# One-core Fourier mixing and SwiGLU kernel: weight columns loaded by thirds, odd folds moved, od copies and unit order changed

## The chip, the cores and the metric

The kernel runs on one core of a Trainium2 chip. The core has five engines, each with its own stream of instructions: TensorE (PE, matrix products), VectorE (DVE), ScalarE (ACT), GpSimd (POOL) and SyncE (SP, which here only issues transfers). They wait for each other by semaphores, and transfers between the chip's memory (HBM) and the core's memory (SBUF) run beside them on 16 DMA engines. The metric is the device time of one execution in microseconds (us); less is better. Three executions of the kernel before took 606.0, 605.89 and 604.55 us, with a median of 605.89 us.

## The reference

```python
X = np.fft.fft(x, axis=1)            # x: (8, 3008, 256)
X = np.fft.fft(X, axis=2)
h = X.real.reshape(8 * 3008, 256)
g = h @ w_gate                       # (256, 1536)
silu = g * (1.0 / (1.0 + np.exp(-g)))
out = (silu * (h @ w_val)) @ w_out   # (1536, 256)
```

The input is taken through a Fourier transform over the 3008 rows of each of the 8 batches and another over the 256 channels; only the real part is kept. Each of the 24064 resulting rows then goes through a gated block with 1536 hidden columns.

## The kernel before

The real part of the double transform is a product of cosines minus a product of sines. Row k of a batch is P - Q and row M - k is P + Q, with P the cosine part and Q the sine part, so the kernel computes P and Q for half of the rows (12032 of them) and derives both rows of a pair. The channel transform is never applied to the rows: it is multiplied into the weights. On TensorE, 256 x 256 tables of cosines (CD) and sines (SDt) are multiplied with the raw gate and value weights, and the results are copied to Wp and Wq; Wm is Wq times a column m2 that is -2 except at one place. This is done in thirds of 512 of the 1536 columns. The first third is made in the written-out beginning (`first_w`, line 490; `double`, line 499), the other two inside the planned part (`weight_op`, line 1746), one product at a time: gate cosine, gate sine, value cosine, value sine.

The 12032 half rows are cut into 24 tiles of 320 to 512. A unit is a tile t and one of twelve slices f of 128 hidden columns, 288 units in all. In tile 0 and in two units of tile 1 a unit is "whole": gate and value each get a product with Wp on P, one with Wq on Q, and, after SiLU on ScalarE and a product on VectorE (lines 1320 and 1323) have used that sum, one with Wm on Q for the mirrored row (SiLU in line 1341, product in line 1344). All these products are recorded in line 1285. The other units share the work differently (marks in `KINDS`), with products also on GpSimd (lines 1496, 1505 and 1508). The last product with w_out is line 1549, and rows leave by SP's queue (line 1562).

The seven later batches are loaded by SP's queue, folded by GpSimd (lines 174 to 198) and transformed on TensorE (line 1708) while the units of earlier tiles run. Batch 1's part C is loaded into XC and its part A into XA.

The beginning is written out by hand and runs in program order on every engine. Batch 0 is loaded (lines 251 to 260), its falling rows are put in order by a product with a permutation (`place`, line 422), and rows are added crosswise (`cross`, line 435; `cross_halves`, line 438). Then the 256 channels are folded to 128, with a sum for the even half (eo = 0) and a difference for the odd half (eo = 1): on GpSimd for segments 0 and 1 (`fold_d`, line 484), on VectorE for segments 2 and 3 (`half_fold`, line 448). TensorE multiplies the folds with the tables of the row transform (`half_folded`, line 473; `folded_c`, line 479). ScalarE copies one half of each result to a tile called od (`even_copy`, line 598), and VectorE writes P and Q of the first tiles as sum and difference with it (`first_puts`, line 603).

The raw weights are loaded by GpSimd's own queue, in four transfers that also convert to bf16. `load_w(True)` takes the first 512 columns of gate and value (line 375) to W0; `load_w(False)` takes the other 1024 columns (line 377) to Wraw. Wraw lies over the first half of XA, which is free once `place` has read it; kfO and rrO, angles for a table, lie over the second half. A tile of zeros that two transfers on SP copy into XC (line 633) is set by GpSimd in line 396; SP's loads of batch 1 stand behind these two.

Everything after the beginning is recorded as operations with an engine, a duration and dependences, and a planner (`Sched.run`, line 1123) puts them in order: each engine takes, within a window of nominal times, the operation that can start first. The nominal time of an operation is the sum of the TensorE work recorded before it plus a shift by its kind (`SHIFT`) and by tile and kind (`BIAS`). The planner is told when engines come free at the beginning (line 1948) and when the later weights have landed:

```python
S.add("DMA", 0.01, lambda: None, w=[(("W",), (fc, gv))], lat=1.5 * gv)
...
S.run({'DVE': 1.6, 'ACT': 1.2, 'POOL': 3.3, 'PE': 0.0, 'SP': 1.0})
```

The planner's times decide the order only. On the chip each engine executes its stream in that order and waits for what is not ready.

Of the kernel before, what the change touches and what calls it, by code (L numbers as in the profile page):

```python
# [19 lines left out]
def kernel(  # L20
# [211 lines left out]
    FA = tp.tile([P, 2, 2, D], F32, name="FA")  # L232
    FL = tp.tile([P, 2, 2, P], F32, name="FL")
# [162 lines left out]
    nc.gpsimd.memset(zeros, 0.0)  # L396
    ce_angle = [[tp.tile([P, 2, NCE], F32, name=f"{nm}{ch}") for nm in ("rr", "ra")] for ch in range(2)]
    tp.tile([P, 4916], F32, name="pad")
# [85 lines left out]
    def fold_d(eo):  # L484
        ptt(EOA[:, eo, 0:2, :, 0:P], FA[:, :, :, P:0:-1], FA[:, :, :, P:D], op=SUMS[eo])

# [15 lines left out]
    X3c = XC.rearrange("p a q d -> p (a q d)")  # L502
    psG.at = psV.at = 2
# [25 lines left out]
    half_folded(1, 2, True)  # L529
    half_folded(1, 0, False)  # L530
# [3 lines left out]
    load_w(0)  # L534
    cross_halves(FC[:, 0], XC0, psC, 0)
    half_fold(0, EB[:, 0, 0], FC[:, 0], psC, 0)
# [61 lines left out]
    def even_copy(eo):  # L598
        od = odp.tile([P, NCE], F32, name="od")
        nc.scalar.copy(od, acc[eo][0][:, 0:NCE])  # L600
        return od

# [11 lines left out]
    copies[0]()  # L614
    od0 = even_copy(0)
# [60 lines left out]
    def rows(r0, n, step):  # L676
# [33 lines left out]
    BIAS = {  # L710
        (18, 'VM'): -3.25,
        (16, 'EG'): -3.75,
        (18, 'HP'): -3.7,
        (17, 'HP'): 3.3,
        (23, 'PUT'): 3.5,
        (23, 'HP'): -2.1,
        (23, 'OD'): 5,
        (23, 'EV'): 0.4,
        (5, 'ROW'): -4.75,
        (17, 'VM'): 3.35,  # L720
        (18, 'EG'): -3.4,
        (18, 'VAL'): 1.3,
        (19, 'EG'): 0.75,
        (19, 'VAL'): 1.35,
        (19, 'ROW'): 4.45,
        (19, 'FOLD'): -2.7,
        (19, 'HP'): -1.1,
        (21, 'HP'): -1.15,
        (20, 'SEED'): -0.95,
        (20, 'HP'): -2.1,  # L730
        (20, 'VM'): -1.85,
        (22, 'VAL'): 5,
        (5, 'SM'): 3.15,
        (11, 'SEED'): -4.25,
        (13, 'VM'): -2.25,
        (13, 'HP'): -5,
        (16, 'OD'): -3.3,
        (16, 'VM'): -2.6,
        (15, 'HM'): 1.95,
        (15, 'EV'): -1.05,  # L740
        (16, 'ES'): 1.8,
        (16, 'HM'): -3.5,
        (1, 'SM'): -0.85,
        (4, 'SM'): -4.35,
        (5, 'ES'): 5,
        (11, 'HP'): 1.35,
        (13, 'SP'): 2.15,
        (13, 'EV'): 4,
        (0, 'SM'): 0.8,
        (0, 'EG'): 2.25,  # L750
        (0, 'VG'): 2.7,
        (0, 'PUT'): -0.25,
        (0, 'ROW'): -1.35,
        (0, 'HG'): -0.9,
        (0, 'EV'): 1.1,
        (0, 'HP'): -0.9,
        (0, 'VM'): 2.7,
        (0, 'FOLD'): -3.75,
        (0, 'GM'): 0.85,
        (0, 'HM'): -2.35,  # L760
        (0, 'SEED'): -0.1,
        (0, 'OD'): -0.35,
        (1, 'FOLD'): 2.35,
        (1, 'HP'): -2.15,
        (1, 'ROW'): 0.05,
        (1, 'PUT'): -1.05,
        (1, 'VG'): -0.15,
        (1, 'HG'): -0.5,
        (1, 'GM'): 0.5,
        (1, 'VM'): -2.35,  # L770
        (1, 'OD'): -0.65,
        (1, 'EG'): -0.6,
        (1, 'SEED'): 0.3,
        (1, 'ES'): -0.5,
        (1, 'HM'): 0.6,
        (1, 'EV'): 0.1,
        (2, 'EG'): -4.75,
        (2, 'SP'): -4.0,
        (2, 'VG'): 0.85,
        (2, 'SEED'): -1.25,  # L780
        (2, 'HM'): -0.8,
        (2, 'PUT'): 1.35,
        (2, 'ES'): -0.65,
        (2, 'GM'): 0.9,
        (2, 'FOLD'): -0.9,
        (2, 'OD'): 0.5,
        (2, 'HG'): 0.5,
        (2, 'EV'): -1.5,
# [1190 lines left out]
```

## Time and profile before

| | us |
|---|---|
| three executions: median (lowest to highest) | 605.89 (604.55 to 606.0) |
| the profiled execution: its time | 606.75 |
| its span, first to last instruction | 605.0 |
| PE busy in the span | 594.0 |
| DVE busy | 572.4 |
| ACT busy | 561.4 |
| POOL busy | 513.7 |

The mean granted TensorE clock of the profiled execution is 0.997 of full speed. An instruction's time runs from its start to its end; matmuls overlap, so successive starts say more on PE's pace than durations do. In the views of the trace, a number in brackets with "x" counts instructions, and a group's "idle before" is the time for which its engine stood still ahead of it, with the instruction or the transfer that ended the wait. Times are from the start of the span, and names of lines are those of this kernel.

### The profile page before, as it was taken

What the parts mean: (1) busy time and instruction counts of PE and PEld (TensorE: products, weight loads), DVE (VectorE), ACT (ScalarE), POOL (GpSimd) and SP (SyncE); (2) the same over time, 40 slices, a digit from 0 to 9 for tenths busy, and PEclk for the clock granted to TensorE, in tenths of its full rate; (3) what the DMA queues carried; (4) which work ended last, traced back from release to release, by engine and by line L of the source; (5) the groups of instructions that cost most, each with busy time, mean ns of one, the idle gap of its engine ahead of it and who ended that gap; (6) DMA issues with size and microseconds to landing.
All of it is one profiled execution on the core that took longest, in us unless ns stands there. A gap on an engine that the chain in (4) does not pass through costs nothing.

```text
span 605.0 us, 12523 instructions
## 1 busy us (share of the span) xinstructions
PE 594.0 (98%) x4015; PEld 390.4 (65%) x4015; DVE 572.4 (95%) x1070; ACT 561.4 (93%) x1086; POOL 513.7 (85%) x463
## 2 busy tenths in 40 slices
PE   8799999999999999999999999999999999999997
PEld 5246666666666666666666666666666666666686
DVE  8689998999999999999999999999999999999993
ACT  7498999999998999899999999998999999999995
POOL 8554899999889999998999988997899567687772
PEclk9899999999999999999999999999999999999999
DMA  9945446244644513355126122037221111111112
GB/s 236 161 107 121 113 122 179 59 124 122 126 113 107 140 53 119 100 129 161 50 67 170 39 60 81 18 95 179 63 62 37 50 57 45 55 46 54 60 52 80
DMA packets 50554, 57.65 MB, mean 95 GB/s; under 512 B 7267, under 2 KB 37399, under 8 KB 50489
## 3 DMA queue, kind: packets, MB, share of 16 engines
q1 hardware_dynamic: 47449, 53.91, 33.3%
q0 software_dynamic: 2672, 2.36, 2.9%
q8 instruction: 31, 0.51, 0.4%
q10 hardware_dynamic: 368, 0.59, 0.3%
q14 instruction: 34, 0.28, 0.2%
HBM read 29.43 MB, written 24.65 MB: 89 GB/s over the span
## 4 chain that ended last, share of the span: by engine, by line
PE 87%; DMA 4%; DVE 3%; ACT 2%; POOL 2%; issue 1%; SPq 1%; ACTq 0%; DVEq 0%; POOLq 0%
PE o L1549 37%; PE g L1285 25%; PE v L1285 19%; PE g L1708 2%; PE o L1708 2%; DMA XA<-in_moe_w_gate_dram 2%; DMA XA<-in_x_dram 1%; DVE sv L1488 1%; PE o L1756 1%; PE v L1549 1%; POOL hm L1496 1%; DVE hp L1499 1%; DVE es L1422 1%; ACT sv L1472 0%; SPq L156 0%
## 5 line engine op out<-in xcount | busy, mean ns | idle before, releaser
L1496 POOL TENSOR_TENSOR hm<-sv 128x1024 bf16<-128x1024 f32 (+2 forms) x137 | 255.1, 1863 | 49.3 <-DVE sv L1488 21.7
L1488 DVE SCALAR_TENSOR_TENSOR sv<-es,v 128x512 f32<-128x512 f32 (+2 forms) x262 | 174.4, 670 | 7.8 <-PE v L1285 5.3
L1549 PE MATMUL o<-Wo,hm 128*128 128x256 bf16 (+1 forms) x1128 | 163.2, 273 | 0.0
L1549 PE MATMUL o<-Wo,hp 128*128 128x256 bf16 (+1 forms) x1104 | 159.3, 272 | 0.0
L1499 DVE TENSOR_TENSOR hp<-sp,v 128x512 bf16<-128x512 f32 (+2 forms) x236 | 157.2, 670 | 2.1 <-PE v L1285 1.3
L1549 PEld LDWEIGHTS <-hm 128*128 128x128 bf16 (+2 forms) x1140 | 111.8, 98 | 57.4 <-issue 1.3
L1549 PEld LDWEIGHTS <-hp 128*128 128x128 bf16 (+2 forms) x1140 | 111.8, 98 | 55.0 <-issue 1.6
L1472 ACT ACTIVATE sv<-g 128x512 f32<-128x512 f32 (+2 forms) x178 | 117.7, 673 | 4.0 <-PE g L1285 3.1
L1397 ACT ACTIVATE sp<-g 128x512 f32<-128x512 f32 (+2 forms) x178 | 110.7, 623 | 4.5 <-PE g L1285 2.0
L1285 PE MATMUL g<-Pt,Wp 128*128 128x512 bf16 (+2 forms) x288 | 107.8, 375 | 0.0
L1285 PE MATMUL v<-Pt,Wp 128*128 128x512 bf16 (+2 forms) x288 | 106.7, 375 | 0.1
L1358 ACT ACTIVATE v<-bc,w 128x512 f32<-128x512 bf16 (+2 forms) x147 | 105.4, 719 | 1.0 <-DVE hp L1499 0.6
L1285 PE MATMUL g<-Qt,Wq 128*128 128x512 bf16 (+2 forms) x288 | 105.1, 376 | 0.1
L1420 ACT ACTIVATE es<-v 128x512 f32<-128x512 f32 (+2 forms) x147 | 90.5, 620 | 4.5 <-PE v L1285 2.4
L1422 DVE SCALAR_TENSOR_TENSOR es<-bc,w,v 128x512 f32<-128x512 bf16 (+2 forms) x127 | 93.0, 735 | 1.5 <-PE g L1285 0.5
L1285 PEld LDWEIGHTS <-Wp 128*128 128x128 bf16 x576 | 56.3, 98 | 28.1 <-issue 1.2
L1285 PE MATMUL g<-Qt,Wm 128*128 128x512 bf16 (+2 forms) x192 | 72.4, 377 | 0.2 <-ACT sg L1320 0.2
L1401 DVE SCALAR_TENSOR_TENSOR sg<-bc,w,g 128x512 f32<-128x512 bf16 (+2 forms) x96 | 69.3, 722 | 0.3 <-PE g L1285 0.2
L1472 ACT ACTIVATE sv<-sg 128x512 f32<-128x512 f32 (+2 forms) x96 | 66.3, 695 | 0.4 <-DVE sg L1465 0.4
L1469 ACT ACTIVATE sp<-g 128x512 f32<-128x512 f32 (+2 forms) x96 | 59.0, 615 | 6.3 <-DVE sg L1465 5.9
L1465 DVE SCALAR_TENSOR_TENSOR sg<-sg,g 128x512 f32<-128x512 f32 (+2 forms) x96 | 63.5, 661 | 0.4
L1285 PE MATMUL v<-Qt,Wm 128*128 128x512 bf16 (+2 forms) x161 | 60.0, 373 | 0.0
(209 smaller groups left out, 755.9 us busy)
## 6 DMA issues: line engine op xcount, KB each, us to landing
out_dram<-ev SPq DMA_DIRECT2D x96, 128.0 KB
XA<-in_x_dram SPq DMA_DIRECT2D x30, 256.0 KB
XA<-in_x_dram SPq DMA_DIRECT2D x112, 64.0 KB
XC<-in_x_dram SPq DMA_DIRECT2D x28, 120.0 KB
XC<-in_x_dram SPq DMA_DIRECT2D x105, 32.0 KB
bc<-br SPq DMA_DIRECT2D x19, 128.0 KB
St<-Fc SPq DMA_DIRECT2D x12, 128.5 KB
out_dram<-ev SPq DMA_DIRECT2D x12, 120.0 KB
```

Source lines behind the costliest of these rows:

```text
L1285: nc.tensor.matmul(ps[:, :n], Wt[:, gv, fs], src[:, :n], start=start, stop=stop, skip_group_check=True)
L1358: nc.scalar.activation(T_[kv][:, :w], bc[t][:, :w], AF.Copy, scale=w0[:, 1, f:f + 1])
L1397: nc.scalar.activation(sp_to()[:, :w], T_[kg][:, :w], AF.Silu)
L1401: nc.vector.scalar_tensor_tensor(T_[keg][:, :w], bc[t][:, :w], w0[:, 0, f:f + 1], T_[kg][:, :w], op0=Alu.mult, op1=Alu.add)
L1420: nc.scalar.activation(T_[kes][:, :w], T_[kv][:, :w], AF.Copy, scale=2.0 if on_pool(u) > 1 else 1.0)
L1422: nc.vector.scalar_tensor_tensor(T_[kes][:, :w], bc[t][:, :w], w0[:, 1, f:f + 1], T_[kv][:, :w], op0=Alu.mult, op1=Alu.add)
L1465: nc.vector.scalar_tensor_tensor(T_[kgm][:, :w], T_[keg][:, :w], 2.0, T_[kg][:, :w], op0=Alu.mult, op1=Alu.subtract)
L1472: nc.scalar.activation(sv()[:, f % 2, w - 1::-1, 1], T_[kgm if by_dve else kg][:, :w], AF.Silu)
L1488: nc.vector.scalar_tensor_tensor(sv()[:, f % 2, w - 1::-1, 0], T_[kes][:, :w], 2.0, T_[kv][:, :w], op0=Alu.mult, op1=Alu.subtract)
L1496: nc.gpsimd.tensor_tensor(hts_(t)[1][:, f - 1:f + 1, :w], sv()[:, :, :w, 1], sv()[:, :, :w, 0], op=Alu.mult)
L1499: nc.vector.tensor_tensor(hts_(t)[0][:, f, :wp], T_[ksp][:, :wp], T_[kv][:, :wp], op=Alu.mult)
L1549: nc.tensor.matmul(st["ps"][:n, j, :], hts[t][minus][:, f, c:c + n], Wo[:, f, :], start=(f == 0), stop=(f == nF - 1))
```

## The change

The raw weights come in six transfers of 512 columns, by thirds: `load_w(0)` stands where `load_w(True)` stood, `load_w(1)` where `load_w(False)` stood, and `load_w(2)` behind the products of the odd fold of part C. The tile FL is gone, and FA has room for four segments.

For segments 2 and 3, VectorE now makes only the even fold in the first place. ScalarE copies the upper halves of these segments to FA (two new copies). The odd fold is made twice: by VectorE behind part C's even folds, directly to bf16 (which takes the place of a ScalarE conversion), and by GpSimd as a new `fold_d(1, 2)` behind `load_w(2)`, in fp32, for a later use. On TensorE the odd products of segments 2 and 3 move behind the first weight product.

The first od copy stands ahead of the first weight copies. One weight copy (value, cosine) is on VectorE instead of ScalarE. The zeros are set by GpSimd behind the new fold, in place of their early position. Two small VectorE scalings of BBc are on ScalarE. The first half of one angle computation goes from the beginning into the planned part.

In the planned part `BIAS` has new values for all 24 tiles and 17 kinds (as a table of rows), the weights' landing times are four constants, and the free times of DVE, ACT and POOL are 2.8, 3.0 and 6.5. `KINDS` and `SHIFT` are as before, and PE executes the same products.

```diff
-    FA = tp.tile([P, 2, 2, D], F32, name="FA")
-    FL = tp.tile([P, 2, 2, P], F32, name="FL")
+    FA = tp.tile([P, 4, 2, D], F32, name="FA")
...
-    def load_w(first, only=(0, 1)):
+    def load_w(c):
         for i, src in ((0, moe_w_gate), (1, moe_w_val)):
-            if i not in only:
-                continue
-            w_ = src.rearrange("(no p) f -> p no f", p=P)
-            if first:
-                nc.gpsimd.dma_start(out=W0[i], in_=w_[:, :, 0:T])
-            else:
-                nc.gpsimd.dma_start(out=Wraw[i][:, :, 0:Dff - T], in_=w_[:, :, T:Dff])
+            w_ = src.rearrange("(no p) f -> p no f", p=P)[:, :, c * T:(c + 1) * T]
+            nc.gpsimd.dma_start(out=Wraw[i][:, :, (c - 1) * T:c * T] if c else W0[i], in_=w_)
...
-    nc.gpsimd.memset(zeros, 0.0)
...
-    def fold_d(eo):
-        ptt(EOA[:, eo, 0:2, :, 0:P], FA[:, :, :, P:0:-1], FA[:, :, :, P:D], op=SUMS[eo])
+    def fold_d(eo, a0):
+        F = FA[:, a0:a0 + 2]
+        ptt(EOA[:, eo, a0:a0 + 2, :, 0:P], F[:, :, :, P:0:-1], F[:, :, :, P:D], op=SUMS[eo])
...
-    fold_d(0)
-    load_w(1)
-    fold_d(1)
+    fold_d(0, 0)
+    load_w(0)
+    fold_d(1, 0)
     for a in range(2, 4):
-        cross_halves(FL[:, a - 2], XA, psA, a)
+        cross_halves(FA[:, a, :, 1:P + 1], XA, psA, a)
...
     opposite(1)
-    for eo in range(2):
-        for a in range(2, 4):
-            half_fold(eo, EOA[:, eo, a, :, 0:P], FL[:, a - 2], psA, a)
-        half_cast(eo, 2)
+    for a in range(2, 4):
+        nc.scalar.copy(FA[:, a, :, P + 1:D], psA[a][:, :, P + 1:D])
+    for a in range(2, 4):
+        half_fold(0, EOA[:, 0, a, :, 0:P], FA[:, a, :, 1:P + 1], psA, a)
+    half_cast(0, 2)
     half_cast(1, 0)
     half_folded(0, 0, True)
     half_folded(0, 2, False)
-    half_folded(1, 2, True)
-    half_folded(1, 0, False)
+    half_folded(1, 0, True)
...
-    load_w(0)
+    load_w(1)
...
     folded_c(0, 1)
-    for a in range(2):
-        ends(Ec0[:, a], XC0, psC, a)
+    od0 = even_copy(0)
+    ends(Ec0[:, 1], XC0, psC, 1)
+    heads(Ec0[:, 0], Ec0[:, 1], CEc)
+    for a in range(2, 4):
+        half_fold(1, EOb[:, 1, a], FA[:, a, :, 1:P + 1], psA, a)
+    copies = [first_w(0, k, 1, p_.tile([P, T], F32, name=n_)) for k, (p_, n_) in enumerate(((psG, "g"), (psV, "v")))]
+    copies[0]()
+    half_folded(1, 2, False)
     for a in range(2):
         half_fold(1, EB[:, 1, a], FC[:, a], psC, a)
-    heads(Ec0[:, 0], Ec0[:, 1], CEc)
-    copies = [first_w(0, 0, 1, psG.tile([P, T], F32, name="g")), first_w(0, 1, 1, psV.tile([P, T], F32, name="v"))]
     for a in range(2):
         folded_c(1, a)
+    load_w(2)
+    fold_d(1, 2)
+    nc.gpsimd.memset(zeros, 0.0)
...
-    copies[0]()
-    od0 = even_copy(0)
+    first_puts(0, od0, (0,))
     for i in range(2):
         row0(0, i, acc[1][i])
     copies[1]()
     od1 = even_copy(1)
-    first_puts(0, od0, (0,))
+    copies = [first_w(1, k, k, psO.tile([P, T], F32, name="o")) for k in range(2)]
+    copies[0]()
     first_puts(1, od1, (0,))
-    copies = [first_w(1, k, 1, psO.tile([P, T], F32, name="o")) for k in range(2)]
-    copies[0]()
     copies[1]()
...
-    angles(rrO[:, 0], kfO, 0, rrO[:, 0].bitcast(I32), (0,))
     double(0)
     double(1)
     for k in range(2):
-        vts(BBc[:, :, 1, k, 0:1], Ec0[:, 1 - k], scalar1=(nsgn, sgn)[k], scalar2=None, op0=Alu.mult)
+        nc.scalar.activation(BBc[:, :, 1, k, 0:1], Ec0[:, 1 - k], AF.Copy, scale=(nsgn, sgn)[k])
...
-    BIAS = {
-        (18, 'VM'): -3.25,
-        (16, 'EG'): -3.75,
...
-    }
+    BIAS_ROWS = (
+        (16.3, -16.6, -10.55, 11.5, 4, 5.25, -11.2, 14.8, -26.65, 26.8, -5, -20.85, 17.7, 19.2, -4.85, 2.65, -8.5),
...
+    )
+    BIAS = {(t, k): v for t, row in enumerate(BIAS_ROWS) for k, v in zip(SHIFT, row)}
...
+    W_AT = (2.0, 3.2, 4.6, 6.0)
...
-            S.add("DMA", 0.01, lambda: None, w=[(("W",), (fc, gv))], lat=1.5 * gv)
+            S.add("DMA", 0.01, lambda: None, w=[(("W",), (fc, gv))], lat=W_AT[2 * fc - 2 + gv])
...
-    S.run({'DVE': 1.6, 'ACT': 1.2, 'POOL': 3.3, 'PE': 0.0, 'SP': 1.0})
+    S.run({'DVE': 2.8, 'ACT': 3.0, 'POOL': 6.5, 'PE': 0.0, 'SP': 1.0})
```

More of the change, by code (lines that the diff above doesn't have):

```diff
@@ L395 @@
     nc.gpsimd.memset(sel[0:1, :], 1.0)
-    nc.gpsimd.memset(zeros, 0.0)
     ce_angle = [[tp.tile([P, 2, NCE], F32, name=f"{nm}{ch}") for nm in ("rr", "ra")] for ch in range(2)]
-    tp.tile([P, 4916], F32, name="pad")
+    tp.tile([P, 4404], F32, name="pad")
     angles(ce_angle[0][0], kf, 0, ti[0])
@@ L502, with even_copy @@
     X3c = XC.rearrange("p a q d -> p (a q d)")
+    def even_copy(eo):
+        od = odp.tile([P, NCE], F32, name="od")
+        nc.scalar.copy(od, acc[eo][0][:, 0:NCE])
+        return od
     psG.at = psV.at = 2
@@ L533 @@
     heads(hd[:, 0], hd[:, 1], CEa)
-    load_w(0)
+    load_w(1)
     cross_halves(FC[:, 0], XC0, psC, 0)
+    ends(Ec0[:, 0], XC0, psC, 0)
     half_fold(0, EB[:, 0, 0], FC[:, 0], psC, 0)
@@ L596, in products @@
         return res + [(BBc[:, q, eo, k, :], Tab[:, 1, q, (eo + k) % 2, NOO:NTAB], slice(0, G)) for k in range(2)]
[L598 to L601, printed above, removed]
     def first_puts(eo, od, tiles):
@@ L1788, in angle_op @@
     def angle_op(ch):
-        S.add("DVE", 1.1 if ch else 0.6, lambda: angles(rrO[:, ch], kfO, ch, rrO[:, ch].bitcast(I32), (0, 1) if ch else (1,)),
+        S.add("DVE", 1.1, lambda: angles(rrO[:, ch], kfO, ch, rrO[:, ch].bitcast(I32)),
               r=[(("A",), "pre")], w=[(("rr",), ch)])
```

344 lines of the change are left out of this document (removed), and 23 rows, old and new, of the table BIAS_ROWS.

## The prediction

> **What bounds the kernel now.** I read the page first, then PE's waits, PE's timeline around the longest of them, the windows behind it, and the DMA issues.
>
> ```profile
> span 605.0 us, 12523 instructions
> PE 594.0 (98%) x4015; PEld 390.4 (65%) x4015; DVE 572.4 (95%) x1070; ACT 561.4 (93%) x1086; POOL 513.7 (85%) x463
> ```
>
> PE is busy for 594.0 of 605.0 us, so the product stream is the bound and only PE's waits and slow stretches can be won. The profiled execution took 606.75 us, 1.75 outside its span, and is 0.86 above the median of 605.89. The list of PE's waits names one that matters:
>
> ```profile
> PE o L1756 <- DMA XA<-in_moe_w_gate_dram: 4.2, 1, 4.2
> ```
>
> In PE's timeline the wait is followed by a slow stretch:
>
> ```profile
> 20.34 0.37 PE L1285 MATMUL v<-Pt,Wp 128*128 128x480 bf16 x1
> 24.91 0.60 PE L1756 MATMUL o<-XA,CD 128*128 128x512 bf16 x2 [4.20 <-DMA XA<-in_moe_w_gate_dram]
> ...
> 27.83 0.61 PE L1285 MATMUL g<-Pt,Wp 128*128 128x480 bf16 x1
> 28.23 0.61 PE L1285 MATMUL g<-Qt,Wq 128*128 128x480 bf16 x1
> ...
> 29.29 0.37 PE L1285 MATMUL g<-Qt,Wm 128*128 128x480 bf16 x1
> 29.49 0.37 PE L1285 MATMUL v<-Qt,Wm 128*128 128x480 bf16 x1
> ```
>
> Equal products start 0.40 us apart until 29.0 and 0.20 apart from 29.29. The windows give the granted clock (after POOL's column) as 0.50 there, and show that PE stands hardly at all for the next 157 us:
>
> ```profile
> 27.00:28.00 1.00, 1.00 (x4) 0.45 (x3) 1.00 (x3) 0.33 (x1) 0.00 (x0) 0.50 1.41 206
> 42.50:200.00 157.50, 157.50 (x1058) 103.60 (x1058) 151.83 (x272) 148.81 (x287) 143.62 (x132) 1.00 0.48 120
> ```
>
> The weights' issues, with us to landing last:
>
> ```profile
> XA<-in_moe_w_gate_dram POOLq DMA_DIRECT2D x1, 512.0 KB, 10.9
> XA<-in_moe_w_val_dram POOLq DMA_DIRECT2D x1, 512.0 KB, 13.7
> W<-in_moe_w_gate_dram POOLq DMA_DIRECT2D x1, 256.0 KB, 4.2
> W<-in_moe_w_val_dram POOLq DMA_DIRECT2D x1, 256.0 KB, 6.8
> ```
>
> Issued at 10.54, 11.35, 13.92 and 14.65, they land one after the other at 14.7, 18.15, 24.9 and 28.35. PE has products of its own for the first third, but its order puts the second third's first product ahead of the Q products of three units, and there it stands.
>
> **The change part by part.** *What the wait costs today.* The wait is 4.20. From 25.78 to 29.29 PE does seven 480-column products (0.2025 each at the later pace) and one weight pair (0.43), 1.85 of work in 3.51: 1.66 lost. Together 5.86.
>
> *The beginning on PE.* VectorE has the same operations on the way to the last half fold of part C, only in another order, so it ends there at 16.57 as now. The first weight product needs the PSUM of segment 2, now freed by VectorE's odd fold at about 15.6, and starts there instead of at 16.17. By the rows' starts, behind it come its sine pair (to 16.5), four odd products (0.65), the odd part C (0.65), the row heads (0.65) and the value pairs (0.87): PE reaches the first unit at 19.3 (now 19.39). ScalarE's two new copies (about 0.4 each, by the 0.48 of an od copy of 377) lie at 12.0 to 12.8, where it stands for 0.64 today, and a 0.6 conversion goes. VectorE puts P at 16.6, makes the new value copy at 19.05 (0.69) once PE has the product, and puts Q by 20.5 (now 19.6), so PE's five P products, the second waiting some 0.3 for that copy, end at 20.6 with Q just there. If a later Q were not covered by the P products it would cost PE its own 0.9.
>
> *The unit order at the start.* PE now does five Q products before the first weight pair. It asks for the second third's gate at 21.5, its value at 22.8, the last third's gate at 24.1 and value at 27.8 (work between them: 14 products and five pairs in all by 24.5, or 4.99). In today's trace the same 4.99 is done at 30.8 (4 products by 20.5, 0.87 by 25.78, 1.85 by 29.29, 1.49 after). With no wait on weights PE gains 6.3.
>
> *The six loads.* After the first two, four loads of 256 KB follow W's value load, taken to land at 18.15 as now. Bounds: 512 KB in 3.5 (28.35 - 24.86), or 1.75 each, against 3.4 for each load whatever its size (18.15 - 14.74). At the mean rate of today, 1024 KB in 10.2, each takes 2.55. I take 2.15, between the fast end and the mean, because SP's loads of batch 1, which today begin at 12.5 beside the weights, cannot start before GpSimd has set the zeros (below). Landings are then 20.3, 22.45, 24.6 and 26.75: one wait of 0.5, at the third. Ends: 0, and 4.25 at 3.4 each. Two more issues cost GpSimd 0.73 each, ahead of kfO and the angles; VectorE asks for the angles at 22.6, they are made by 20.1.
>
> *ScalarE.* It is full from 30 to 49 today (4.94, 5.00, 4.91 of 5 us), and PE has waited on it at 42.5. Its unit work starts at 25.80 now. In the new order it ends the beginning at 21.5 (first od 15.6, three weight copies, od, doublings 1.34, and two scalings of 0.12 to 0.2 that were VectorE's). From 25.80 to its copy of bc at 49.18 it works 21.8 (23.4 less 1.6 idle), and one more SiLU (0.46) stands ahead of that copy in the new order: 43.8, a gain of 5.4. The wait's idle time was ScalarE's reserve as well; that is why not all of 6.3 is won.
>
> *GpSimd and SP.* Before the zeros GpSimd now has two issues (1.46) and a fold (1.1), so SP's two zero transfers start at about 18.7, not 10.95, and the loads behind them at 20.2, not 12.5. Today 25 issues take until 38.3, at 0.73 each once the weights are in (twelve from 27.8 to 36.5), nine in the 5.7 from 17.23; eight by 25, seventeen at 0.73 and 0.6 of waiting for the last copy make 38.0, and part C to POOL at 42.4 (now 41.77). Its folds (7.1, and the 1.45 that come later today) end at 50.9. Today GpSimd begins its products at 56.54 with 1.45 of these folds still to do, but three memsets (2.2) already done: a gain of 4.9. From 56.5 to 150 GpSimd is busy for 91.4 of 93.5, so it keeps about this lead. What GpSimd loses at first is hidden by today's 7.66 of standing ahead of 56.54; without it every us is a us late.
>
> *The rest.* Every tile has new shifts, so its units' work gets new places, with the same products. PE lost some 0.9 behind 30 us (0.16 at 42.5, 0.68 between 200 and 250, specks). The new order could lose none of it (-0.9), or, at four times today's number of such waits, 2.8 more. I take no difference: the rows say nothing for either side. The end (PE's last products, an eviction, a store) has the same operations.
>
> *The sum.* PE 6.3 - 0.5 = 5.8; ScalarE 5.4; GpSimd 4.9, with some room since only one of PE's waits today (0.6 at 248) leads back to it. The slowest decides, so 5.1, between the last two. 606.75 - 5.1 = 601.65 for a profiled execution, 600.8 against the median.
>
> **A rule of the Trainium skill.** Behind PE's short waits of 1.04, 0.51 and 0.38 the clock stayed full; behind 4.20 it was half for 3.4. A wait near 2 lies between and is not shown. The Trainium skill, "TensorE: Matmul & The Clock Gate", Part 1, says that the clock halves after an idle window of about 3.4 us and comes back after as long a busy one; the trace agrees for 4.20. By it a rest wait of 2 us costs only itself; without it up to 1.66 more.
>
> **The rivals.** *Everything moves at PE's pace* (0.14): ScalarE and GpSimd keep up and the later 0.68 and 0.07 go too: 6.3 + 0.75, or 598.8. For it: ScalarE has idle time again at 53. Against it: its 19 full us.
>
> *Loads paced by their number* (0.12). If each takes 3.4 us, they land at 21.55, 24.95, 28.35 and 31.75; PE waits 2.15 and 2.05, 4.25 with the first speck, and gains 2.0: 603.9. For it: W's value load took as long as a load of twice the size. Against it: that one ran beside SP's loads at a DMA share over 1. The Trainium skill, "DMA: Bandwidth & Descriptors", Anatomy of one DMA, speaks for this rival: about 2.0 us fixed per such transfer beside its bytes, so that two more loads would cost 4 us if nothing overlapped. The trace is no clear help, as today's intervals of 3.4, 6.7 and 3.5 do not follow size.
>
> *The new order waits more later* (0.10): 2.8 more behind 30 us, 603.6.
>
> *Batch 1 comes late* (0.08), the case on the other side. If SP's whole delay of 6.2 (18.7 - 12.5) reaches the landing of part C, GpSimd folds from 48 to 56.5 and, with the memsets still ahead of it, is 0.75 behind today. Batch 1's first transform stands today directly behind its fold (fold ends 89.1, product at 89.4), so PE, 5.9 ahead, would stand there more than 5 us, lose the gain and another 1.66 of half clock: 605.9 + 0.75 + 1.66 = 608.3. It decides from a delay of about 5.4 on. Against it: SP's issues have a pace of 0.73 without the weights beside them.
>
> **How the numbers follow.** The forecast has 0.56, with a range of its own from 599.6 to 602.3. About 0.3%, 1.8 us, is what a measurement of this kernel can tell from no change. Faster by more (below 604.1): 0.56 + 0.14 + 0.09 of the loads + 0.07 of the later waits = 0.86. Within: 0.03 + 0.03 + 0.01 = 0.07. Slower (above 607.7): 0.07 of late batch 1. The range from 598.5 to 604.5 takes in the first four cases and leaves out late batch 1 and the tails.
>
> **What would show it.** Right: PE's first unit near 19.3; no wait over 1 us at the weight products, and a granted clock of 1.00 from 20 to 30; four landings by 27; SP's first load of batch 1 near 20; ScalarE's bc copy near 44; GpSimd's fold of part C from 42 and its first product of units near 51 to 52. Wrong would be: PE waits over 1 us on XA's loads, GpSimd starting part C after 44, PE standing ahead of batch 1's transform, or PE idle of more than 2 us in all behind 45.

## The result, and the profile after

The changed kernel takes 603.41 us (median of 8 executions, 602.72 to 604.19) against 606.05 (8 executions, 604.25 to 608.18) for the kernel before. The ratio is 0.9955, with a 95% interval from 0.9937 to 0.9973. It is faster, by 2.6 us, where 5.1 was forecast. The time lies within the stated range, 598.5 to 604.5, and above the forecast's own, 599.6 to 602.3. The profiled execution took 604.19 us with a span of 602.4; it is the slowest of the eight, 0.78 above their median. Its clock is 0.999.

The page of the changed kernel, first lines:

```profile
span 602.4 us, 12460 instructions
PE 590.4 (98%) x3954; PEld 390.3 (65%) x4015; DVE 572.5 (95%) x1069; ACT 562.0 (93%) x1088; POOL 516.8 (86%) x466
```

The trace lacks 61 of PE's 4015 products, so PE's own busy time is a few us short here. The weight loads (PEld) are complete, and the comparisons of progress below use their starts.

The list of PE's waits; each line names PE's tile and line, what it waited for, and us in total, times, longest:

```profile
PE o L292 <- DVE sel L247: 1.0, 1, 1.0
PE g L964 <- DVE Pt L612: 0.8, 1, 0.8
PE g L964 <- ACT sv L1151: 0.5, 1, 0.5
PE v L470 <- ACT EOb L482: 0.5, 1, 0.5
PE g L964 <- ACT sg L999: 0.5, 1, 0.5
...
```

The wait of 4.2 us on XA's load is gone, and no transfer is left in the list. In its place stand waits of at most 0.8, all on VectorE and ScalarE; the 1.0 on sel, ahead of the first transform, is as before. The windows, whose columns are the busy times of PE, PEld, DVE, ACT and POOL and then the granted clock and the DMA share, show that the half clock went with it:

```profile
27.00:28.00 1.00, 0.95 (x5) 0.46 (x5) 1.00 (x2) 1.00 (x3) 0.87 (x2) 1.00 0.23 57
```

The issues of the four later loads, with us to landing last:

```profile
XA<-in_moe_w_gate_dram POOLq DMA_DIRECT2D x1, 256.0 KB, 4.0
XA<-in_moe_w_val_dram POOLq DMA_DIRECT2D x1, 256.0 KB, 4.6
XA<-in_moe_w_gate_dram POOLq DMA_DIRECT2D x1, 256.0 KB, 5.3
XA<-in_moe_w_val_dram POOLq DMA_DIRECT2D x1, 256.0 KB, 6.6
```

They are issued at 13.78, 14.50, 15.91 and 16.63, so they land at 17.8, 19.1, 21.2 and 23.2. PE asks for the first of them only at 23.17. So both costs of the old wait were removed, 5.86 us together, and 3.3 of that were lost elsewhere. Three places in the profile show where.

First the beginning, in PE's timeline (start, duration, and the wait ahead in brackets):

```profile
13.59 0.49 PE L470 MATMUL v<-Tab,EOb 128*128 128x377 bf16 x2 [0.45 <-ACT EOb L482]
19.78 0.37 PE L964 MATMUL g<-Pt,Wp 128*128 128x480 bf16 x1
20.30 0.38 PE L964 MATMUL v<-Pt,Wp 128*128 128x480 bf16 x1 [0.15 <-DVE Wp L490]
21.47 0.38 PE L964 MATMUL g<-Pt,Wp 128*128 128x480 bf16 x1 [0.79 <-DVE Pt L612]
22.16 0.37 PE L964 MATMUL g<-Qt,Wq 128*128 128x480 bf16 x1
```

The first unit comes at 19.78 and the Q products at 22.16. Second, ScalarE's timeline: its first unit work comes at 22.69, and the bc copy, the mark that the prediction took for ScalarE, comes at 46.13 for 49.18. It is 3.05 earlier. First its row in the kernel before, then two rows of the changed kernel:

```profile
49.18 0.59 ACT L1883 CAST bc<-g 128x512 bf16<-128x512 f32 x1 [0.37 <-PE g L1879]
```

```profile
22.69 1.03 ACT L999 ACTIVATE sg<-g 128x480 f32<-128x480 f32 x2 [0.51 <-POOL XA L343]
46.13 0.58 ACT L1562 CAST bc<-g 128x512 bf16<-128x512 f32 x1
```

Third, GpSimd's timeline with the folds of batch 1, of part C (in XC) and then of part A (in XA), in the kernel before and in the changed kernel:

```profile
41.77 2.35 POOL L174 TENSOR_TENSOR SDf<-XC 128x1020 f32<-128x1020 f32 x1 [1.96 <-DMA XA<-in_x_dram]
64.49 2.35 POOL L174 TENSOR_TENSOR SDf<-XA 128x1020 f32<-128x1020 f32 x1
```

```profile
45.85 2.35 POOL L174 TENSOR_TENSOR SDf<-XC 128x1020 f32<-128x1020 f32 x1 [12.33 <-PE g L1558]
61.92 2.36 POOL L174 TENSOR_TENSOR SDf<-XA 128x1020 f32<-128x1020 f32 x1 [0.43 <-DMA out_dram<-ev]
```

The fold of part C is 4.1 us later than before. The first fold of XA is 2.57 earlier, about the 2.6 that the kernel gained.

What PE has won at each moment is seen when the starts of its weight loads are set side by side by the product columns done. This table is worked out from the traces. The left column is a time in the profiled run of the kernel before. The others say by how many us the kernel had the same number of columns done earlier than the last product that the kernel before had begun by then. Each column is one execution, so a few tenths mean little:

| at | changed | zeros late alone | old beginning, new order | new beginning, old order | zeros later still |
|---|---|---|---|---|---|
| 20 | -0.5 | 0.6 | 0.5 | -0.5 | 0.9 |
| 31 | 4.5 | 5.1 | 6.0 | 4.7 | 5.4 |
| 41 | 3.1 | 5.0 | 4.8 | 4.4 | 5.3 |
| 60 | 3.0 | 5.0 | 4.8 | 4.4 | 5.3 |
| 95 | 0.8 | 5.0 | 3.3 | 2.8 | 3.5 |
| 250 | 1.9 | 5.3 | 4.8 | 3.0 | 3.7 |
| 598 | 2.4 | 5.4 | 4.6 | 3.2 | 3.9 |

The four columns on the right are experiments, below. The changed kernel wins 4.5 us by 31, loses 1.4 by 41 and 2.2 from 60 to 95, and gets 1.1 back by 250. The part of each step is what the experiments were made for.

### The profile page after: what moved, and what is told of

Read it like the earlier page. It is cut to its first block, busy times and chain, and to the rows that moved or that the text cites. A ratio compares the mean times of both kernels' runs of the same rounds, so it can differ in the third digit from the quotient of the medians.

```text
span 602.4 us, 12460 instructions
## 1 busy us (share of the span) xinstructions
PE 590.4 (98%) x3954; PEld 390.3 (65%) x4015; DVE 572.5 (95%) x1069; ACT 562.0 (93%) x1088; POOL 516.8 (86%) x466
## 4 chain that ended last, share of the span: by engine, by line
PE 86%; POOL 4%; DVE 3%; ACT 3%; issue 2%; DMA 2%; SPq 0%; POOLq 0%; ACTq 0%; DVEq 0%
PE o L1228 37%; PE g L964 23%; PE v L964 19%; PE g L1387 2%; PE o L1387 2%; DMA XA<-in_x_dram 1%; POOL hm L1175 1%; PE v L1228 1%; DVE sv L1167 1%; ACT sv L1151 0%; ACT v L1037 0%; PE o L1435 0%; ACT es L1099 0%; POOL SDf L174 0%; DVE es L1101 0%
## 5 line engine op out<-in xcount | busy, mean ns | idle before, releaser
L964 PE MATMUL v<-Pt,Wp 128*128 128x512 bf16 (+2 forms) x286 | 104.7, 375 | 1.4 <-DVE sv L1167 0.3
L964 PE MATMUL g<-Pt,Wp 128*128 128x512 bf16 (+2 forms) x276 | 103.2, 374 | 1.5 <-DVE Pt L612 0.8
L964 PE MATMUL g<-Qt,Wq 128*128 128x512 bf16 (+2 forms) x246 | 89.5, 374 | 0.7
L964 PE MATMUL v<-Qt,Wm 128*128 128x512 bf16 (+2 forms) x160 | 59.6, 373 | 0.6 <-DVE hp L1002 0.2
```

The source lines that it names most:

```text
L964: nc.tensor.matmul(ps[:, :n], Wt[:, gv, fs], src[:, :n], start=start, stop=stop, skip_group_check=True)
```

## The experiments

Two theories of where the gain comes from stood at the start. By the first, the thirds bring it, since PE gets each piece of the weights when it asks for it. By the second, the late zeros alone make it: SP's loads of batch 1 wait for the zeros, so they are no longer beside the weights. Both left open what took half of the gain: the new beginning, the new order of the units, or GpSimd, which gets batch 1 later.

In the recorded expectations the second theory is called C. The first is called A, but in the expectation of the first experiment A is GpSimd's lateness and B is the new order. The ledger named there is the table above, and e3_zeros_late_alone is the kernel of its column "zeros late alone". The kernels under one heading share the runs of the kernel before, whose median stands in the heading. These medians go from 606.05 to 606.78, so under different headings a ratio and a difference of medians can disagree by 0.7 us.

### The zeros and the thirds, each alone (before: 606.78)

The changed kernel with the zeros back at their old place, ahead of the weights:

```diff
     nc.gpsimd.memset(sel[0:1, :], 1.0)
+    nc.gpsimd.memset(zeros, 0.0)
...
     fold_d(1, 2)
-    nc.gpsimd.memset(zeros, 0.0)
```

> The changed kernel with one edit: GpSimd sets the zeros at their old place, so that SP's loads of batch 1 start near 12.5 us as before the change, not at 20.3. Theory A (the late loads keep GpSimd idle until 45.85 and its lateness costs PE some 2.4 us between 56 and 95): GpSimd starts part C of batch 1 near 41.5, PE is 2 us or more further by 95, and the time falls from 603.4 to 600.8 to 601.6. Theory B (the waits belong to the new order of the units itself): GpSimd starts earlier, but PE's waits between 56 and 95 stay and the time is 603.0 to 603.8. Theory C (the late zeros are what lets the weights land early): the last third's gate lands after 24, PE waits for it more than 1 us, and the time is 603 to 605.

It took 605.14 us (603.53 to 607.35), a ratio of 0.9968 (0.9951 to 0.9984). SP's loads begin at 12.1 for 20.3. GpSimd folds part C at 42.99, 2.9 earlier, and yet the time does not fall as A had it; it lies just above the range of C. The second third's issues at 13.81 and 14.54, and the list of PE's waits:

```profile
XA<-in_moe_w_gate_dram POOLq DMA_DIRECT2D x1, 256.0 KB, 10.2
XA<-in_moe_w_val_dram POOLq DMA_DIRECT2D x1, 256.0 KB, 12.4
```

```profile
PE o L488 <- DMA W<-in_moe_w_val_dram: 2.1, 1, 2.1
PE o L1435 <- DMA XA<-in_moe_w_gate_dram: 0.6, 1, 0.6
```

The same loads of 256 KB land 10.2 and 12.4 us after issue, for 4.0 and 4.6 with late zeros, and W's value load takes 10.2 for 4.8. PE waits on weights again, although they come by thirds. By the ratios the late zeros are worth 0.8 us in the changed kernel (0.9968 to 0.9955) and by the medians 1.7, with intervals that overlap.

The kernel before with the weights in six loads, and nothing else (`load_w` is rewritten as in the change, which is left out here):

```diff
...
-    load_w(1)
+    load_w(0)
...
-    load_w(0)
+    load_w(1)
+    load_w(2)
```

> The kernel before with one edit: the weights behind the first third come in four loads of 512 columns, issued one after the other where the two large ones stood. Everything else, the order of the units too, is the old one, and SP's loads of batch 1 still run beside them from 12.5. Theory A (the thirds alone take PE's wait and the half clock behind it away): the second third's gate lands at 20.5 to 21.5, PE waits for it less than 1 us, the granted clock stays 1.00 from 20 to 30, and the time falls from 606.05 to 601 to 602.5. Theory C (SP's loads beside them hold the weights up, whatever their size): it lands at 22.5 or later, PE waits 2 us or more, time 603.5 to 606.

It took 604.22 us (602.27 to 605.41), 0.996 (0.9945 to 0.9974). PE still waits on XA's first load, 3.4 us for 4.2, and still has the half clock behind it:

```profile
PE o L1752 <- DMA XA<-in_moe_w_gate_dram: 3.4, 1, 3.4
```

```profile
25.00:26.00 1.00, 1.00 (x4) 0.44 (x3) 1.00 (x3) 0.82 (x2) 0.00 (x0) 0.50 0.96 118
```

A first load of half the bytes lands at 24.0 for 24.9, and 0.4 of that is an earlier issue: it is the traffic beside it that sets its time, more than its size. Still, by the ratio the thirds alone bring 2.4 us. The profiled execution, the slowest of twelve, shows 1.2 of them.

The kernel before with one line moved, the zeros set behind part C's heads:

```diff
-    nc.gpsimd.memset(zeros, 0.0)
...
     for a in range(2):
         folded_c(1, a)
+    nc.gpsimd.memset(zeros, 0.0)
```

> The kernel before with one edit: GpSimd sets the zeros behind part C's heads, near 16.3, so that SP's loads of batch 1 start near 18 instead of 12.5. The weights still come in two small and two large loads, in the old order of units. Theory C (SP's loads hold the weights up): the second large gate load, of 512 KB, lands near 20 instead of 24.9, PE's wait nearly goes, and the time falls to 602 to 603.5, with GpSimd later at batch 1. Theory A (the size of the loads is what counts): it lands at 22.5 to 24, PE still waits 2 to 3.5 us, time 604 to 606.

It took 601.34 us (600.83 to 601.69), 0.9906 (0.9886 to 0.9926). By the ratio it gains 5.7 us. That beats the kernel before and the changed one, and it is more than was expected of it. The issues, SP's first loads, PE's waits, and the folds of batch 1 (views: issues, SP's queue, PE's waits, GpSimd's timeline):

```profile
XA<-in_moe_w_gate_dram POOLq DMA_DIRECT2D x1, 512.0 KB, 5.7
XA<-in_moe_w_val_dram POOLq DMA_DIRECT2D x1, 512.0 KB, 8.2
```

```profile
16.01 1.49 SPq L633 DMA_DIRECT2D XC<-Af  x2
17.54 0.83 SPq L151 DMA_DIRECT2D XC<-in_x_dram  x2
```

```profile
PE g L1285 <- ACT sg L1320: 1.5, 2, 1.4
```

```profile
42.11 2.35 POOL L174 TENSOR_TENSOR SDf<-XC 128x1020 f32<-128x1020 f32 x1 [7.30 <-DMA XA<-in_x_dram]
59.49 2.35 POOL L174 TENSOR_TENSOR SDf<-XA 128x1020 f32<-128x1020 f32 x1
```

The large loads land 5.7 and 8.2 us after issue for 10.9 and 13.7, with their size unchanged. PE wins 5 us by 31 and keeps them to the end. SP's loads start 5 us later than before, and yet part C is folded at 42.11 for 41.77 and XA at 59.49 for 64.49: SP's last copy into part C is issued at 37.68 for 37.39, so the later start costs SP only 0.3.

The changed kernel with two loads of 1024 columns in place of the four thirds behind the first:

```diff
-    load_w(2)
...
-            w_ = src.rearrange("(no p) f -> p no f", p=P)[:, :, c * T:(c + 1) * T]
-            nc.gpsimd.dma_start(out=Wraw[i][:, :, (c - 1) * T:c * T] if c else W0[i], in_=w_)
+            w_ = src.rearrange("(no p) f -> p no f", p=P)[:, :, T:Dff] if c else src.rearrange("(no p) f -> p no f", p=P)[:, :, 0:T]
+            nc.gpsimd.dma_start(out=Wraw[i][:, :, 0:Dff - T] if c else W0[i], in_=w_)
```

> The changed kernel with one edit: behind the first third the weights come in two loads of 1024 columns again, both where the second third's loads stand; two issues on GpSimd go, so the zeros are set some 1.5 us earlier. Theory C (not the thirds but the absence of SP's loads lets the weights land early): the gate lands near 19.5 and the value near 23, both before PE asks (23.2 and 24.6), and the time is 603.4 or up to 0.5 less, as SP starts earlier. Theory A (the thirds are needed): the gate lands after 23.5, PE waits 1 us or more, and the time is 604.5 or more.

It took 603.14 us (602.29 to 603.49), 0.9933 (0.9915 to 0.9952), the same as the changed kernel within the intervals. With late zeros the thirds are worth nothing that shows. So the second theory holds for late zeros: they need no thirds, and alone they bring over twice what the thirds bring alone. The first is not empty: with early zeros the thirds bring 2.4 us, but they add nothing to late zeros.

### What gave the rest back (before: 606.66)

The kernel with late zeros alone, with the new shifts of the units (and the release times of weights and engines that go with them, and the angles whole in the planned part):

```diff
-    BIAS = {
...
+    BIAS_ROWS = (
...
-            S.add("DMA", 0.01, lambda: None, w=[(("W",), (fc, gv))], lat=1.5 * gv)
+            S.add("DMA", 0.01, lambda: None, w=[(("W",), (fc, gv))], lat=W_AT[2 * fc - 2 + gv])
...
-    S.run({'DVE': 1.6, 'ACT': 1.2, 'POOL': 3.3, 'PE': 0.0, 'SP': 1.0})
+    S.run({'DVE': 2.8, 'ACT': 3.0, 'POOL': 6.5, 'PE': 0.0, 'SP': 1.0})
```

> This is the kernel of e3_zeros_late_alone (601.34) with the changed kernel's shifts of the units' order, its release times of the weights and its start times, and nothing else: two large loads, the old beginning, the zeros set behind part C's heads. If the new order is what gives back the 2.1 us between e3 and the changed kernel: 602.5 to 603.5, with GpSimd's fold of part C at 42 as in e3 and the ledger of PE's progress falling behind e3 from 31 us on. If the order is harmless and the beginning or GpSimd's lateness is the cause: 600.8 to 601.8.

It took 602.35 us (602.01 to 602.67), 0.9926 (0.9905 to 0.9946), which lies between the two expectations. Against late zeros alone the ratios differ by 0.0020, 1.2 us, and the table's last row by 0.8, with intervals that overlap. The table shows a loss and a gain under this small sum: from 31 to 95 the new order loses 2.7 us (6.0 to 3.3) where the old one loses 0.1, and by 250 it has 1.4 of them back where the old one gains 0.3. PE's waits in the first of these stretches:

```profile
33.25 0.36 PE L964 MATMUL g<-Qt,Wm 128*128 128x480 bf16 x1 [0.46 <-ACT sg L999]
37.88 0.36 PE L964 MATMUL v<-Qt,Wm 128*128 128x480 bf16 x1 [0.17 <-DVE hp L1002]
```

The changed kernel has the same two, 0.45 and 0.16, at 35.01 and 39.63. The same two products wait with either beginning, and no transfer is behind it. The other part of the loss comes between 60 and 95, though XA's fold is there as early as with late zeros alone (59.49, above):

```profile
59.35 2.37 POOL L174 TENSOR_TENSOR SDf<-XA 128x1020 f32<-128x1020 f32 x1
```

The changed kernel with the old shifts, release times and angle, so the new beginning alone:

```diff
-    BIAS_ROWS = (
...
+    BIAS = {
...
-    S.run({'DVE': 2.8, 'ACT': 3.0, 'POOL': 6.5, 'PE': 0.0, 'SP': 1.0})
+    S.run({'DVE': 1.6, 'ACT': 1.2, 'POOL': 3.3, 'PE': 0.0, 'SP': 1.0})
```

> This is the changed kernel with the old shifts of the units' order, the old release and start times: the six loads, the new beginning and the zeros behind it stay. If the new beginning (PE's first unit 0.4 late, Q products later) and the zeros at 18.4 (GpSimd's fold of part C at 45.9 for 42) give back the 2.1 us: 602.5 to 604. If the order gives it back: 600.8 to 601.8. In the old order PE asks for the second third's gate product near 21, ahead of the Q products, and its load lands at 17.8, so no wait on a load in either case.

It took 603.63 us (603.07 to 604.18), 0.9944 (0.9925 to 0.9964): the new beginning alone, thirds and all, gives back 2.3 us of what late zeros bring (the table's last row: 2.2). One part is there at once (4.7 for 5.1 at 31, and 4.4 for 5.0 at 41), the other comes from 60 to 95, where it loses 1.6 and the old beginning nothing. There PE waits on ScalarE, and ScalarE on GpSimd's hm products (those for the mirrored rows), whose chain starts late:

```profile
61.78 2.36 POOL L174 TENSOR_TENSOR SDf<-XA 128x1020 f32<-128x1020 f32 x1 [1.05 <-DMA XC<-in_x_dram]
```

```profile
66.18 0.64 ACT L1472 ACTIVATE sv<-g 128x512 f32<-128x512 f32 x1 [0.77 <-POOL hm L1496]
66.87 0.38 PE L1285 MATMUL g<-Pt,Wp 128*128 128x512 bf16 x1 [0.56 <-ACT sv L1472]
84.78 0.38 PE L1285 MATMUL g<-Pt,Wp 128*128 128x512 bf16 x1 [0.43 <-ACT sv L1472]
```

The changed kernel with the zeros ahead of the last third's issues:

```diff
+    nc.gpsimd.memset(zeros, 0.0)
     load_w(2)
     fold_d(1, 2)
-    nc.gpsimd.memset(zeros, 0.0)
```

> This is the changed kernel with only the setting of the zeros moved ahead of the two issues of the last third, from 18.4 to about 15.9. SP's loads should start near 17.5 for 20.3 and GpSimd's fold of part C near 43 for 45.85. If GpSimd's lateness is what costs PE some 1.4 us between 85 and 95: 601.5 to 602.3, and VectorE's and ScalarE's waits of 0.7 on the hm products near 82 and 88 gone. If it costs nothing that matters: 603.0 to 603.8. The last third's loads now lie beside SP's loads and may take 8 to 10 us to land instead of 5 to 6.6, which would be 25 to 27, about when PE asks for them (23.2 and 26); a wait there of up to 2 us would hide the gain.

It took 602.91 us (602.6 to 603.48), 0.9935 (0.9911 to 0.9959): 1.2 better than the changed kernel by the ratios, not told apart by the intervals, and just below the range given for no effect. SP's loads begin at 17.9 and its last copy into part C is issued at 39.14, but the copy's fold still comes only at 45.45, and XA's fold moves from 61.92 to 61.06. So this step brought GpSimd 0.9 us for the 2.9 that were expected, and tells little of what lateness costs. The loads of the last third did not suffer: PE does not wait on any.

The changed kernel with the value copy of the first weights on ScalarE again:

```diff
-    copies = [first_w(1, k, k, psO.tile([P, T], F32, name="o")) for k in range(2)]
+    copies = [first_w(1, k, 1, psO.tile([P, T], F32, name="o")) for k in range(2)]
```

> This is the changed kernel with the second cosine weight copy (value) on ScalarE, as before the change, instead of on VectorE. VectorE's puts of Q should come 0.7 earlier and PE's wait of 0.79 at its third P product go; ScalarE gets 0.6 more ahead of its unit work, which starts at 22.7 and would start near 23.3. If VectorE's lateness in the beginning sets the pace: 602.5 to 603.0. If ScalarE, full from there to about 45, sets it: 603.4 to 604.2.

It took 603.44 us (602.52 to 603.72), 0.9936 (0.9912 to 0.996), in the range given for ScalarE setting the pace. PE's wait of 0.79 at the third P product goes, and worked out as in the table PE is 1.1 further than the changed kernel at 29 us. At 31 only 0.2 are left, and a new wait has come:

```profile
26.06 0.36 PE L964 MATMUL v<-Qt,Wm 128*128 128x480 bf16 x1 [0.78 <-DVE hp L1002]
```

Neither engine had room for the copy: what one is spared, the other is late by. The median is that of the changed kernel (603.41); the ratio is some 1.2 us better, as it is for the two large loads and for the zeros ahead of the last third, each time with overlapping intervals.

### GpSimd's lateness alone, and thirds with late zeros (before: 606.52)

The kernel with late zeros alone, the zeros set still later, behind the second set of turns (19.2 on SP's queue for 16.0):

```diff
     for a in range(2):
         folded_c(1, a)
-    nc.gpsimd.memset(zeros, 0.0)
...
+    row_signs()
+    turns(rrO[:, 1].bitcast(I32), kfO, 1)
+    nc.gpsimd.memset(zeros, 0.0)
     for hi in range(2):
         q.dma_start(out=X3c[64 * hi + NCR:64 * hi + 64, :].rearrange("p (c d) -> p c d", d=D),
...
-    row_signs()
-    turns(rrO[:, 1].bitcast(I32), kfO, 1)
```

> This is the kernel of e3_zeros_late_alone (old beginning, old order, two large loads) with the zeros set still later, behind the second set of turns: near 19.4 on GpSimd for 15.7, so that SP's loads of batch 1 begin near 21.2 for 17.5 and GpSimd's fold of part C comes near 45.5 to 46.5 for 42.1. Nothing else moves, so it prices GpSimd's lateness alone. If a late part C costs PE what the ledger loses between 65 and 95 us in the kernel with the new beginning and the old order (1.5): 602.4 to 603.4. If that loss belongs to the new beginning and not to part C: 600.9 to 601.7, as e3.

It took 603.27 us (602.89 to 604.19), 0.9951 (0.9932 to 0.9971), in the range given for a late part C. By the medians two fifths of the gain are gone (3.25 for 5.44 us), by the ratios half of it, with one line moved 3 us further. Up to 60 us PE is as far as with the zeros at 15.7, or further; from 60 to 95 it loses 1.8. GpSimd's fold of XA, and the waits behind it on ScalarE and PE:

```profile
45.79 2.36 POOL L174 TENSOR_TENSOR SDf<-XC 128x1020 f32<-128x1020 f32 x1 [11.26 <-DMA XA<-in_x_dram]
61.14 2.35 POOL L174 TENSOR_TENSOR SDf<-XA 128x1020 f32<-128x1020 f32 x1 [1.85 <-DMA out_dram<-ev]
```

```profile
65.53 0.64 ACT L1472 ACTIVATE sv<-g 128x512 f32<-128x512 f32 x1 [1.11 <-POOL hm L1496]
66.22 0.38 PE L1285 MATMUL g<-Pt,Wp 128*128 128x512 bf16 x1 [0.92 <-ACT sv L1472]
84.12 0.38 PE L1285 MATMUL g<-Pt,Wp 128*128 128x512 bf16 x1 [0.43 <-ACT sv L1472]
```

This is the pattern of the new beginning with the old order, with the old beginning. GpSimd stands 1.85 us ahead of XA's fold, is busy without a stop behind it, and PE waits 0.92 and 0.43 on what it makes. The releaser that is named is a store, but the fold reads XA. SP issues XA's last load (L138) at 55.92 here, at 55.94 with the new beginning and the old order and at 51.75 with late zeros alone; the fold comes 5.2 and 5.8 us behind it in the first two, and without a wait in the third.

The kernel with late zeros alone, with six loads (the edit is that of the thirds alone):

> This is the kernel of e3_zeros_late_alone with the six loads of 512 columns, issued where the two large ones are; the two more issues move the zeros on GpSimd from 15.7 to about 17.0 and SP's loads to about 18.8. If the thirds are worth something once the zeros are late (PE's first product of the second third has its weights earlier): 600.3 to 601.0. If not, as the pair of the changed kernel with thirds and with two large loads says: 601.0 to 602.0, the upper end if 1.3 us of lateness on SP costs.

It took 601.56 us (601.14 to 603.79), 0.9926 (0.99 to 0.9951): with the zeros late, the thirds bring nothing that shows, and the time is in the range given for that. Against late zeros alone the median is 0.2 us worse and the ratio 1.2, with intervals that overlap. In the profiled execution, 0.9 above the median, PE is level with late zeros alone at 95 us (5.0 in the table's terms) and 1.1 behind at 598. The zeros are at 17.0 here, and part C is folded later still than in the kernel before this one, at 46.16, without harm up to 95 us. XA's last load is issued at 53.45, and the fold comes on time:

```profile
59.63 2.34 POOL L174 TENSOR_TENSOR SDf<-XA 128x1020 f32<-128x1020 f32 x1
```

So in the old order the time that counts is that of XA's fold, not of part C's. A fold at 59.5 to 59.6 costs PE nothing from 60 to 95, and one at 61.1 or 61.8 costs 1.8 or 1.6 us. In the new order a fold at 59.35 came with a loss of 1.5, so there the fold's time is not the whole cause.

## Why the prediction was right in its sign and wrong in its size

The mechanism held in its main part: the wait of 4.20 and the half clock behind it went, and what was left, 2.6 us, is near the leads that GpSimd and ScalarE kept and not near PE's 4.5 at 31 us. The forecast of 5.1 took the terms as ScalarE 5.4 and GpSimd 4.9. They measured 3.05 (the bc copy at 46.13) and 2.57 (XA's fold at 61.92), and the kernel gained 2.6. The step that failed is the size of these two terms. That the time still fell into the stated range is in part luck: its upper end was set for two rivals, and one of them, loads paced by their number, did not come, while the other, the new order, accounts for some 1 us. The beginning on PE and the pace of SP, which took the rest, were in no rival at their size.

*The six loads.* The cause was put down to two things at once, the thirds and the absence of SP's loads; the size was taken from rows with SP's loads beside them. The loads landed 1.3 to 2.1 us apart rather than 2.15, W's value load at 16.0 rather than 18.15, and all were in by 23.2 rather than 26.75. The wait of 0.5 that was forecast did not come. With the zeros late the thirds add nothing, as the two pairs with and without them show. The rival of loads paced by their number at 3.4 us each fell. The Trainium skill, "DMA: Bandwidth & Descriptors", Anatomy of one DMA, gives some 2.0 us fixed to each such transfer; no run here shows that this adds up over loads that overlap, as six loads in place of four cost nothing that the intervals tell.

*The beginning on PE.* It was forecast as nearly free: first unit at 19.3, Q ready at 20.5. It measured 19.78 and 22.16. Two waits were not in the working. VectorE waits for ScalarE's new FA copies ahead of its even folds, and ScalarE's conversion of EOb and PE's products wait in turn, PE 0.45 at 13.59:

```profile
12.13 0.42 DVE L442 TENSOR_TENSOR EOA<-FA,g 128x256 f32<-128x256 f32 x1 [0.64 <-ACT FA L522]
```

And the third P product needs a PSUM slot that VectorE frees only after the puts of tile 1, which come behind the value copy and Q's puts: 0.79 at 21.47. The working counted the work on PE and the time of Q, and left out who holds the slots. The old beginning with late zeros has its first unit at 18.79.

*ScalarE.* It was to begin unit work at 21.5 and began at 22.69, as the beginning was late. The 1.6 us of idle time in its stretch up to the bc copy was to vanish. It is busy for 21.98 of the 23.44 us from 22.69 to 46.13, so 1.46 of it stayed. It was taken for a mark of the late loads, and it is there without them.

*GpSimd and SP.* The start of SP's loads was right (20.3 for 20.2), the pace was not. Eight issues were forecast by 25, and three were out: the first two took 4.37 us (L151 at 20.30), while the weights still landed. Such a pair stands in the rows of the kernel before, but the working passed over it. It counted nine issues in the 5.7 us from 17.23, and the rows have seven there; they are nine only with the first two, which took 4.71 from 12.48. The pair before and in the changed kernel:

```profile
12.48 4.71 SPq L151 DMA_DIRECT2D XC<-in_x_dram  x2
```

```profile
20.30 4.37 SPq L151 DMA_DIRECT2D XC<-in_x_dram  x2
```

The last copy was issued at 41.41 for 38.0 and part C folded at 45.85 for 42.4, which the prediction had named as a sign of its own error ("after 44"). GpSimd's first product of units came at 54.26 for 51 to 52. That a lateness of GpSimd counts in full once it is full, as the prediction said, fits the zeros set still later: XA's fold comes 1.65 later than with late zeros alone, and PE loses 1.8. What was not seen is where it counts: at the fold of XA, which SP loads behind part C, and not at part C's.

*The rest.* The new order was taken as no difference, with a rival of 2.8 more of waits. It loses 2.7 from 31 to 95 with the old beginning, and then wins part of it back, so that 0.8 to 1.2 are left, which the intervals do not tell from nothing. It was priced at nothing because no row spoke for either side. Why it does better between 95 and 250 was not tried.

*The sum.* Late zeros alone bring 5.4 us by the medians (606.78 to 601.34). The new beginning costs 2.3 of them and the new order 1.2 when each is added alone. Together they cost 1.8 by the medians of late zeros alone and of the changed kernel with two large loads, which were run side by side, and 3.0 by the ratio of the changed kernel itself. By the first of these they do not add up, and the table says why that can be: each alone loses some 1.5 in the same stretch from 60 to 95. The profiled execution of the changed kernel loses 2.2 there, the three variants nearest to it (two large loads, zeros before the last third, value copy on ScalarE) 1.3 to 1.5. GpSimd stands 0.43 at XA's fold in the first and not in the others, which would fit, but this was only read and not tried.

*Rivals.* "Batch 1 comes late" was described as a mechanism with its own sign: it did happen, at its mechanism (SP's delay reaching GpSimd) but with a smaller price, because the delay of part C was 4.1 us and not over 5.4, and because it met PE as waits of half a us on hm, not as one long stand ahead of the transform. It did not decide the sign; it took much of the size. "Everything at PE's pace" needed ScalarE and GpSimd to keep up, and came near only where neither the beginning nor the order was changed.

## What to carry to other kernels

Ask of each late transfer what shares the DMA engines with it, before cutting it into pieces: moving one memset, on which another queue's loads waited, brought over twice what six loads in place of four brought, the loads added nothing to it, and moving the same memset 3 us further lost two fifths of its gain again. When a long stall is taken out, the next limit is whoever used it as reserve; list for each engine the first instruction that would stand, with what it waits for, and price the slots that hold PE as well as the work. A new order of the work should be compared with the old one on its own, in the state without the stall: here the old one did no worse.

## What the runs showed of the hardware

- Loads of one queue are slowed by another queue's, here to 1.4 to 2.7 times their time. W's value load of 256 KB took 4.7 to 5.3 us with SP's loads held back, and 6.8, 7.5 and 10.2 with them beside it; the second third's value load took 4.6 for 12.4; the 512 KB of XA's gate took 5.7 for 10.9. The Trainium skill, "DMA: Bandwidth & Descriptors", Queues, rings and completion order, says that each DMA engine takes turns between the queues that have work for it, one packet at a time. The trace agrees in that GpSimd's loads slow down beside SP's; how the turns are shared was not measured.
- SP's issues are slow at times while the weights land. Its first two loads took 4.37 us to issue at 20.30 in the changed kernel, and later pairs 0.8. With late zeros alone the first two took 0.83 at 17.54, with weights landing too, and the next two loads in line 151 took 3.06 at 19.38, so what holds an issue was not shown. There SP could start 5 us later than before and still issue its last copy within 0.3 us of the time before.
- A stand of PE of 1.38 us (late zeros alone, at 23.15) and one of 2.06 (zeros early, at 21.46) left the granted clock at 1.00; stands of 3.38 (thirds alone) and 4.20 halved it for 3.4 us. That narrows the gap between 1.04 and 4.20 that the prediction left open to 2.06 to 3.38. It agrees with the idle window of about 3.4 us in the Trainium skill, "TensorE: Matmul & The Clock Gate", Part 1.
- The time from SP's last copy to part C's fold was not fixed: 3.5 us from the end of its issue with late zeros alone and in the changed kernel, 5.4 with the zeros ahead of the last third and 6.0 with thirds and late zeros. What made it longer was not tried.
